# Two attention and GLU layers for one decode step: the first attention's V product made wide, its score mask and q block made one matmul each, and the places at the change of stage dealt anew

## The chip, the cores and the metric

The kernel runs on one core of one Trainium2 chip. The metric is the device time of one execution in microseconds (us). The core has five engines with a queue of their own each: TensorE (PE, with its weight loads shown apart as PEld), VectorE (DVE), ScalarE (ACT), GpSimd (POOL) and SyncE (SP), which here only issues transfers. Sixteen DMA engines move the data from HBM to the on-chip memory (SBUF). Matmuls write to PSUM, eight banks of 512 fp32 per partition.

## The reference

Four sequences, one new token each (x is 4 x 512), go through attention, GLU, attention, GLU, with the same weights and caches both times:

```python
W = min(4096, max(256, Sk // 4))            # 2048 of the 8192 cached places
q = (x @ wq).reshape(B, 1, 32, 128)          # 32 query heads, 8 key heads: 4 share one
scores = q . k[last W] * Dh ** -0.5
o = softmax(scores) . v[last W]
attn = o.reshape(B, 1, 4096) @ wo
glu = (sigmoid(g) * u) @ w_down              # g = x @ w_gate, u = x @ w_up, F = 1792
x = x + attn(layernorm(x)); x = x + glu(layernorm(x)); and both once more
```

All tensors are bf16. One pass needs K and V of the window, 16.8 MB each, wq and wo 4.2 MB each, and three GLU matrices of 1.8 MB each.

## The kernel before, in words

**Places.** SBUF holds 50 slots of 4 KB per partition (`arena`). Slots 0 to 31 hold K of all eight heads, four slots a head in two tiles (`kpair`): K is read once, turned in place on DVE and used by both attentions. The other 18 slots are nine tiles of 8 KB, through which everything else goes: wq, wo (four tiles, kept from the first attention to the second), V (two tiles a head, one for each pair of sequences) and the GLU's matrices. A tile is given back when its last reader is done (`done`), and the next load of the list takes it. Around the change from the first attention to the GLU and on to the second attention, loads of half a tile are used (`load_half`), and each has a fixed home in a table (`homes`): a half of the tiles named Y and Z (V of head 7), GA (first V tile of head 6), WQ (first tile of wq) or SP, which is the small scratch `side`. Parts of V of heads 6 and 7 and of wq stay for the second attention. One V tile of head 7 is parked in PSUM during the GLU: DVE transposes copy it there (`stash`, L578, and `stash_half`, L600) and back (L593, L606).

**Order.** All loads go out on SP's queue in one fixed order (`loads`, issued at L401); SP waits at each load until the last reader of its place is done, so a load that waits holds up all behind it. Every compute step is an operation of a planner (`_Plan`), with what it reads, writes and which PSUM banks it uses. `_schedule` orders the steps of each engine by estimated costs, and engines run their steps strictly in that order. From the end of the first GLU on, PE's steps keep the order in which they are written (`P.chain`).

**One head of the first attention.** DVE turns K in four pieces (L887). `q_unit`: four matmuls with a shifted eye `eyew` (L875) spread the head's q over a block, ACT copies it to `qbd` (L880). `softmax_unit`: four matmuls write the mask to four groups of 32 partitions of a bank (L905), 16 more add the scores (L916); DVE takes the maxima (L929 to L941), ACT the exponentials (L944). `turn_p`: one matmul permutes them (L957), ACT copies (L959), DVE transposes (L964) to `ebuf`. `sums_old`: POOL splits the sums into three bf16 parts (L973 to L977), PE spreads them (L983), DVE inverts (L990). `pv_unit`: 32 matmuls of 128 x 8 for each V tile, with V as the weights (L1006), so the first tile can be used and given back before the second lands; then DVE (L1014), PE (L1024), DVE (L1029), and `wo_unit` (L1195), 16 matmuls of 128 x 16.

**One head of the second attention, heads 7 to 1,** takes the wide path. `pv_wide`: 16 matmuls with the exponentials as weights and V streamed 512 wide (L1088), which need both V tiles; then on DVE a transpose (L1097), a reduction (L1102) and a shift (L1104), on POOL a sum and a product with the inverse sums (L1106, L1109); `o_back`: two small matmuls (L1123) and an ACT copy (L1129); `wo_wide`: four matmuls 512 wide (L1142), added up over the heads in one bank and turned back once (`wo_copy` L1169, `wo_back` L1179), or `wo_compact`: 16 small ones (L1158). The sums take one fp32 matmul (L1064) between POOL steps (L1059, L1069). The wide path's buffers lie in a slot that wq has left (`wide_buffers`).

**The GLU** multiplies with w_gate and w_up, four loads each (L1379), and with w_down (L1420, L1445).

Of the kernel before, what the change touches and what calls it, by code (L numbers as in the profile page):

```python
# [6 lines left out]
F32 = mybir.dt.float32  # L7
# [271 lines left out]
def build(nc, A_x, A_k, A_v, A_wq, A_wo, B_wg, B_wu, B_wd, out, cfg=None):  # L279
# [45 lines left out]
    with es:  # L325
# [12 lines left out]
        eyew = sb("eyew", [128, 224], BF16)  # L338
# [4 lines left out]
        msk_s = sb("msk_s", [128, 32], BF16)  # L343
# [178 lines left out]
        def load_wq(k):  # L522
# [3 lines left out]
            else:  # L526
                for i in (1, 0):
                    for c in range(i, NC):
                        load_half(("wq", c, k, i), wq_d[:, c, i * SLOT:(i + 1) * SLOT], "bw_4k", SLOT,
                                  (((Y, 0), (Y, 1), (WQ, 1), (WQ, 0)), (None, (WQ, 0), (GA, 0), (SP, 0)))[i][c])  # L530
# [23 lines left out]
        def load_glu(k):  # L554
            for nm, src, two in (("wg", wg_d, wg_p), ("wu", wu_d, wu_p)):
                if k == 0:
                    for c in range(NC):
                        load_half((nm, c, k), src[:, c, :], "bw_3k", F,
                                  (((WQ, 0), (GA, 0), (SP, 0), (Y, 0)), ((Y, 1), (Z, 0), (WQ, 0), (GA, 0)))[nm == "wu"][c])
# [3 lines left out]
            for n, (a, b) in enumerate(bounds_of(k)):  # L563
                if k == 0:
                    load_half(("wd", a, k), wd_d[:, a:b, :].rearrange("p k n -> p (k n)"), "bw_4k", (b - a) * D,
                              ((SP, 0), (Y, 0), (Y, 1), (Z, 0))[n])
# [42 lines left out]
        def load_v(h, bp, k, n_use):  # L609
            name = ("V", h, bp, k)  # L610
            tiles = {(HKV - 2, 0): ((GA, 0),), (HKV - 3, 1): ((Y, 0), (Y, 1))}.get((h, bp)) if k else None
# [20 lines left out]
        def keep_wq(s):  # L632
            hfree.add(s)
# [13 lines left out]
        P.op("gpsimd", "eyew0", 200.0, lambda g: g.memset(eyew[:], 0.0), w=[("eyew0",)])  # L647
# [4 lines left out]
        for jh in range(2):  # L652
            for bp in range(2):
                for i in range(2):
# [10 lines left out]
             lambda g: g.affine_select(msk_s[:, :].rearrange("p (i y) -> p i y", i=2),  # L665
                                       ones_f[:, :].rearrange("p (i y) -> p i y", i=2),
                                       [[1, 2], [0, NR]], ALU.is_equal, 0.0, base=-1, channel_multiplier=1),
# [15 lines left out]
             lambda v: v.tensor_reduce(eyew[:, 96:128], ident.rearrange("p (a j) -> p j a", a=4), AXX, ALU.max),  # L683
             r=[("e", 0), ("eyew0",)], w=[("eyew",)])
# [6 lines left out]
        ey = eyew[:, 96:128]  # L691
# [11 lines left out]
        P.op("vector", "selw", 100.0, lambda v: v.tensor_copy(selw[:, :], eyew[:, 96:96 + NB]), r=[("eyew",)], w=[("selw",)])  # L703
# [163 lines left out]
        def q_unit(tag, h, k2):  # L867
            hh = h % 4
            src = qh[32 * hh:32 * hh + 32, h // 4 * 64:h // 4 * 64 + 64].rearrange("p (x r) -> p x r", r=REP)
            dst = ps[:, CB, 0:256].rearrange("p (x y) -> p x y", y=NR)  # L870

            def e_qx(pe):
                last = None
                for a in range(4):
                    last = pe.matmul(dst[:, :, a * REP:(a + 1) * REP], eyew[32 * hh:32 * hh + 32, 96 - 32 * a:224 - 32 * a],  # L875
                                     src, start=True, stop=True)
                return last
            P.op("tensor", "qx" + tag, 250.0, e_qx, r=[("qh", h // 4), ("eyew",)], w=[("cb",)], banks=(CB,))
            P.op("scalar", "qe" + tag, c_act(256),
                 lambda a: a.copy(qbd[:, k2 * 256:(k2 + 1) * 256], ps[:, CB, 0:256]),  # L880
                 r=[("cb",)], w=[("q", k2)], banks=(CB,))
# [12 lines left out]
        def softmax_unit(tag, hk, wait=False, q=True, between=None):  # L894
# [7 lines left out]
            def e_m(pe):  # L902
                last = None
                for gi in range(4):
                    last = pe.matmul(ps[32 * gi:32 * gi + 32, bank, :], msk_s[:, :],  # L905
                                     msk_m[:, :].unsqueeze(1).broadcast_to([128, 256, 2]), start=True, stop=False)
                return last

            def e_s(pe):
                last = None if wait else e_m(pe)  # L910
                for cp in range(4):
                    for gi in range(4):
# [4 lines left out]
                                         kt[:, cp // 2, cp % 2, jh * NJ:(jh + 1) * NJ, :], start=False, stop=(cp == 3))  # L917
# [37 lines left out]
        def turn_p(L, tag, k2, pb, wide=False):  # L955
# [10 lines left out]
            if L == 0:  # L966
                sums_old(tag, k2)
# [70 lines left out]
        def wide_buffers(slots, op):  # L1038
# [15 lines left out]
            rest["op"] = op  # L1054

# [518 lines left out]
```

## Time and profile before

| | |
|---|---|
| median of 3 runs | 177.51 us (177.5 to 178.89) |
| the profiled execution | 177.0 us, of which the span of the instructions is 175.3 |
| read from HBM | 69.73 MB, 398 GB/s over the span |
| busy: PE, PEld, DVE, ACT, POOL | 105.7, 54.7, 104.4, 32.7, 22.2 us |
| matmuls | 1661, and as many weight loads |
| first attention: K transposes | 32 of 1205 ns |
| V products: L1006, L1088 | 576 matmuls, 18.2 us; 112 matmuls, 7.3 us |

In the profile, L12 is line 12 of the kernel before. A group of instructions is told as line, engine, operation, what it writes and reads, how often, and then busy time and mean duration. The page's section 2 cuts the span into 40 slices; a digit is the busy share in tenths. In the chain of work, each piece has its start, its length and what it was, followed back from the last instruction to whatever released it. A "DMA" piece is time in which the chain waited for a transfer. In answers by windows, the columns are the window, its length, the busy time and number of instructions of each engine, the granted PE clock, the DMA share and GB/s. In an answer on one line, the three numbers are the least, middle and greatest duration in ns, then the first and last start in us.

### The profile page before, as it was taken

The numbers are of one execution on the slowest core, as the hardware profiler recorded it, in microseconds if no ns is written. First come the engines' busy times: TensorE is split into PE (matmuls) and PEld (weight loads), VectorE is DVE, ScalarE is ACT, GpSimd is POOL, SyncE is SP. The second block draws the span as 40 slices with busy tenths as digits, with TensorE's granted clock in tenths as the row PEclk, the third lists the DMA queues.
The fourth block names the chain that finished last, engine by engine and source line by source line (L and its number), as shares of the span: only waits on it lengthen the run. The fifth ranks groups of instructions, "written<-read, shape, count | busy, mean of one in ns | idle before, by whom it ended". The sixth has DMA issues, their size and how long they took to land.

```text
span 175.3 us, 3927 instructions
## 1 busy us (share of the span) xinstructions
PE 105.7 (60%) x1661; PEld 54.7 (31%) x1661; DVE 104.4 (60%) x257; ACT 32.7 (19%) x87; POOL 22.2 (13%) x90
## 2 busy tenths in 40 slices
PE   0536246259566273661765456547977999776673
PEld 0203112014334041340445452142322444445321
DVE  6307997994957738378322381316299999751351
ACT  2002031322303003021030000100143455430011
POOL 6100010101101001010010000000011453442000
PEclk9999999999999999999999999999999999995555
DMA  5999999999999999999999999999999999999980
GB/s 188 426 426 426 426 419 424 408 421 423 419 419 412 420 424 426 421 405 427 419 419 415 415 400 407 402 410 403 394 413 404 423 419 424 421 416 423 419 344 25
DMA packets 12226, 70.00 MB, mean 399 GB/s; under 512 B 1320, under 2 KB 1328, under 8 KB 6064
## 3 DMA queue, kind: packets, MB, share of 16 engines
q1 hardware_dynamic: 12200, 69.74, 97.1%
q8 instruction: 13, 0.21, 0.5%
q14 instruction: 5, 0.04, 0.1%
q10 hardware_dynamic: 8, 0.00, 0.0%
HBM read 69.73 MB, written 0.00 MB: 398 GB/s over the span
## 4 chain that ended last, share of the span: by engine, by line
DMA 52%; DVE 24%; PE 19%; issue 2%; SPq 1%; ACT 0%; DVEq 0%
DMA arena<-in_A_v_cache_dram 20%; DMA arena<-in_B_w_down_dram 18%; DVE arena L887 12%; DMA arena<-in_A_wq_dram 10%; PE ps L916 8%; DMA arena<-in_B_w_gate_dram 5%; DVE small L929 3%; PE ps L905 3%; PE ps L1088 2%; DVE small L933 1%; DVE arena L593 1%; PE ps L1006 1%; DVE side L937 1%; PE ps L828 1%; DVE small L941 1%
## 5 line engine op out<-in xcount | busy, mean ns | idle before, releaser
L887 DVE STREAM_TRANSPOSE arena<-arena 128x1024 f32<-128x1024 f32 x32 | 37.0, 1205 | 0.1
L1006 PE MATMUL ps<-side,arena 128*128 128x8 bf16 x576 | 18.2, 168 | 14.1 <-DMA arena<-in_A_v_cache_dram 14.0
L916 PE MATMUL ps<-arena,side 128*32 128x512 bf16 x256 | 25.0, 524 | 0.1
L1006 PEld LDWEIGHTS ps<-side,arena 128*128 128x128 bf16 x576 | 16.7, 104 | 20.5 <-DMA arena<-in_A_v_cache_dram 18.8
L929 DVE TENSOR_REDUCE small<-ps 128x1 f32<-128x512 f32 x16 | 10.8, 676 | 17.6 <-PE ps L916 17.5
L944 ACT ACTIVATE side<-ps,small 128x512 bf16<-128x512 f32 x16 | 11.0, 687 | 36.8 <-PE ps L1024 18.3
L905 PE MATMUL ps<-small,msk_s 128*32 128x512 bf16 x64 | 8.4, 512 | 13.9 <-DVE arena L887 13.1
L880 ACT CAST side<-ps 128x256 bf16<-128x256 f32 x16 | 5.9, 370 | 34.4 <-PE ps L916 25.4
L959 ACT CAST side<-ps 128x512 bf16<-128x512 f32 x16 | 9.4, 586 | 10.8 <-PE ps L957 10.8
L916 PEld LDWEIGHTS ps<-arena,side 128*32 128x32 bf16 x256 | 8.2, 119 | 10.0 <-issue 7.2
L973 POOL CAST small<-small 128x1 bf16<-128x1 f32 x9 | 1.7, 188 | 76.1 <-ACT side L944 76.1
L957 PE MATMUL ps<-side,perm 128*128 128x512 bf16 x16 | 7.9, 494 | 5.2 <-ACT side L944 5.2
L828 PE MATMUL ps<-arena,xn 128*4 128x512 bf16 x60 | 7.5, 572 | 3.9 <-DMA arena<-in_A_wq_dram 3.6
L784 ACT ACTIVATE small<-ps 128x4 f32<-128x4 f32 x4 | 0.7, 174 | 48.1 <-PE ps L780 48.1
L1379 PE MATMUL ps<-arena,xn 128*4 128x448 bf16 x60 | 7.2, 549 | 3.3 <-DMA arena<-in_B_w_up_dram 1.5
L964 DVE STREAM_TRANSPOSE side<-side 128x256 f32<-128x256 f32 x16 | 6.9, 433 | 2.0 <-ACT side L959 1.8
L875 PE MATMUL ps<-side,eyew 32*128 32x64 bf16 x64 | 5.6, 217 | 3.4 <-ACT side L880 2.4
L1088 PE MATMUL ps<-arena,side 128*32 128x512 bf16 x112 | 7.3, 381 | 0.2 <-DVE small L941 0.2
L1014 DVE TENSOR_TENSOR onb<-ps,rinv 128x16 bf16<-128x16 f32 x9 | 1.7, 185 | 9.0 <-PE ps L1006 8.8
L905 PEld LDWEIGHTS ps<-small,msk_s 128*32 128x32 bf16 x64 | 1.7, 97 | 16.8 <-DVE arena L887 15.4
L1388 DVE STREAM_TRANSPOSE side<-ps 128x448 f32<-128x448 f32 x4 | 2.6, 650 | 7.3 <-PE ps L1379 7.3
L840 DVE STREAM_TRANSPOSE side<-ps 128x512 f32<-128x512 f32 x3 | 2.1, 716 | 7.9 <-PE ps L828 7.8
(123 smaller groups left out, 137.8 us busy)
## 6 DMA issues: line engine op xcount, KB each, us to landing
arena<-in_A_v_cache_dram SPq DMA_DIRECT2D x27, 1024.0 KB, 18.8
arena<-in_A_k_cache_dram SPq DMA_DIRECT2D x16, 1024.0 KB, 24.9
arena<-in_A_wq_dram SPq DMA_DIRECT2D x4, 1024.0 KB, 7.8
arena<-in_A_wo_dram SPq DMA_DIRECT2D x3, 1024.0 KB, 26.5
arena<-in_A_wq_dram SPq DMA_DIRECT2D x6, 512.0 KB, 6.3
arena<-in_B_w_up_dram SPq DMA_DIRECT2D x4, 448.0 KB, 6.1
arena<-in_B_w_gate_dram SPq DMA_DIRECT2D x2, 896.0 KB, 21.7
arena<-in_B_w_up_dram SPq DMA_DIRECT2D x2, 896.0 KB, 23.9
```

What stands on the lines that cost most here:

```text
L828: last = pe.matmul(ps[32 * hh:32 * hh + NB, qb, :], xn[:, c * NB:(c + 1) * NB], src[:, o + hh * 512:o + (hh + 1) * 512], start=(c == 0), s ...
L887: P.op("vector", "T%d_%d" % (h, t), c_dve(1024), lambda v, v32=v32: v.transpose(v32, v32), r=[("slot", 4 * h + t)], w=[("slot", 4 * h + t)])
L905: last = pe.matmul(ps[32 * gi:32 * gi + 32, bank, :], msk_s[:, :], msk_m[:, :].unsqueeze(1).broadcast_to([128, 256, 2]), start=True, stop= ...
L916: last = pe.matmul(ps[32 * gi:32 * gi + 32, bank, :], qbd[:, q0:q0 + 32], kt[:, cp // 2, cp % 2, jh * NJ:(jh + 1) * NJ, :], start=False, s ...
L929: lambda v: v.tensor_reduce(nmax[:, k2:k2 + 1], ps[:, bank, :], AXX, ALU.max),
L944: lambda a: a.activation(prow[:, :].rearrange("p (m x t) -> p m x t", x=32, t=2), ps[:, bank, :].rearrange("p (m t x) -> p m x t", x=32, t ...
L957: lambda pe: pe.matmul(ps[:, pb, :], perm[:, :], prow[:, :], start=True, stop=True),
L959: P.op("scalar", "pc" + tag, c_act(512), lambda a: a.copy(prow[:, :], ps[:, pb, :]), r=[("ppb", pb)], w=[("prow",)], banks=(pb,))
L964: P.op("vector", "pt" + tag, c_dve(256), lambda v: v.transpose(et, prow[:, :].bitcast(F32)), r=[("prow",)], w=[("e", k2)])
L1006: last = pe.matmul(ps[:, ob, bp * 8:bp * 8 + 8], src[:, j * 128:(j + 1) * 128], ev[:, j % 2, j % 16 // 2, x0:x0 + 8], start=(j == 0), stop ...
L1088: last = pe.matmul(ps[32 * g:32 * g + 32, ob, :], ew[:, g, mq, t], src.rearrange("p (m t d) -> p t m d", t=2, d=128)[:, t], start=(n == 0) ...
L1379: last = pe.matmul(ps[32 * g:32 * g + NB, gub[n], 0:NF], xn[:, c * NB:(c + 1) * NB], src[:, g * NF:(g + 1) * NF], start=(c == 0), stop=(c ...
```

## The change: what it does

- In the first attention, heads 0 to 6 take the wide V path (`pv_wide`, `sums`, `o_back`); head 7 keeps the old one. Heads 0 to 4 take `wo_wide` and are turned back once, behind head 4; heads 5 and 6 take `wo_compact`.
- The wide path's buffers in the first attention (`first_buffers`) lie in the first half of tile WQ, from the time that wq's first load has been used until head 6's wo (`give(base[WQ])`). Both parities of heads share most of them (`kk = 0`).
- The mask is one matmul over all 128 partitions (`msk_s` is 128 wide), and the q block is one matmul of 128 x 64 with `eye4`, followed by a product on DVE with the mask `maskp` in place of ACT's copy.
- WQ's first half is no longer free at the start of the GLU's loads, so the homes of wq's, w_gate's, w_up's, w_down's and two V loads are dealt anew. The order of the loads and their sizes stay.
- The stash of head 7's tile is tied to head 6's transpose, reduction and shift; head 6's wo comes behind head 7's `pm`.
- In the second attention, one part of wq is multiplied and the second q block made between the first mask and the first scores (`ahead`).

```diff
-                                  (((Y, 0), (Y, 1), (WQ, 1), (WQ, 0)), (None, (WQ, 0), (GA, 0), (SP, 0)))[i][c])
+                                  (((Y, 1), (WQ, 0), (WQ, 1), (GA, 0)), (None, (GA, 0), (Y, 0), (SP, 0)))[i][c])
...
-                                  (((WQ, 0), (GA, 0), (SP, 0), (Y, 0)), ((Y, 1), (Z, 0), (WQ, 0), (GA, 0)))[nm == "wu"][c])
+                                  (((GA, 0), (SP, 0), (Y, 0), (Y, 1)), ((WQ, 0), (Z, 0), (GA, 0), (Y, 0)))[nm == "wu"][c])
...
-                              ((SP, 0), (Y, 0), (Y, 1), (Z, 0))[n])
+                              ((SP, 0), (Y, 1), (WQ, 0), (Z, 0))[n])
...
-            tiles = {(HKV - 2, 0): ((GA, 0),), (HKV - 3, 1): ((Y, 0), (Y, 1))}.get((h, bp)) if k else None
+            tiles = {(HKV - 2, 0): ((Y, 0),), (HKV - 3, 1): ((Y, 1), (WQ, 0))}.get((h, bp)) if k else None
...
         def keep_wq(s):
-            hfree.add(s)
...
         def q_unit(tag, h, k2):
...
-                for a in range(4):
-                    last = pe.matmul(dst[:, :, a * REP:(a + 1) * REP], eyew[32 * hh:32 * hh + 32, 96 - 32 * a:224 - 32 * a],
-                                     src, start=True, stop=True)
...
-            P.op("scalar", "qe" + tag, c_act(256),
-                 lambda a: a.copy(qbd[:, k2 * 256:(k2 + 1) * 256], ps[:, CB, 0:256]),
+                 lambda pe: pe.matmul(dst, eye4[32 * hh:32 * hh + 32, :], src, start=True, stop=True),
...
+            P.op("vector", "qe" + tag, c_dve(256),
+                 lambda v: v.tensor_tensor(
+                     qbd[:, k2 * 256:(k2 + 1) * 256].rearrange("p (x a r) -> p x a r", a=4, r=REP),
+                     dst.rearrange("p (x r) -> p x r", r=REP).unsqueeze(2).broadcast_to([128, NR, 4, REP]),
+                     maskp[:, :].unsqueeze(1).unsqueeze(3).broadcast_to([128, NR, 4, REP]), ALU.mult),
...
             def e_m(pe):
-                for gi in range(4):
-                    last = pe.matmul(ps[32 * gi:32 * gi + 32, bank, :], msk_s[:, :],
-                                     msk_m[:, :].unsqueeze(1).broadcast_to([128, 256, 2]), start=True, stop=False)
+                return pe.matmul(ps[:, bank, :], msk_s[:, :],
+                                 msk_m[:, :].unsqueeze(1).broadcast_to([128, 256, 2]),
+                                 start=True, stop=False, skip_group_check=True)
...
+        def first_buffers(s, op):
+            f = slot_ap(s).bitcast(F32)
+            for k2 in range(2):
+                n = 0
+                for name, size in (("tv", 512), ("o32", 32), ("osh", 32), ("A", 128), ("mb", 64)):
+                    rest[name, k2] = f[:, n:n + size]
+                    n += size
...
         def attn_first():
...
+            first_buffers(base[WQ], named("q0_1_0")[0])
             for h in range(2):
                 front(h)()
+                sum_up(h)
             for h in range(HKV):
                 tag = "0.%d" % h
                 turn = front(h + 2) if h + 2 < HKV else None
+                if h < HKV - 1:
+                    pv_wide(tag, h, h % 2, v_tiles[(0, h)])
+                    if turn is not None:
+                        turn()
+                    if h == HKV - 2:
+                        give(SIDE)
+                    op = late.pop(("tr", tag))()
+                    if h < HKV - 3:
+                        wo_wide(tag, h, op, h % 2, h == 0, h == HKV - 4)
+                    else:
+                        wo_compact(tag, h, op, h % 2)
+                    if h == HKV - 2:
+                        give(base[WQ])
+                    if h == HKV - 4:
+                        wo_copy(0)
+                        wo_back(0, False)
+                    sum_up(h + 2)
+                    continue
                 if h == HKV - 1:
-                    oe, oq = named("oe0.%d" % (h - 1)), named("oq0.%d" % (h - 1))
-                    oe[0].deps.add(stash(stashed, (0, 1)))
-                    oq[0].deps.add(stash(stashed, (2,), oe))
-                    st = stash(stashed, (3,), oq)
+                    rd, sh = named("rd0.%d" % (h - 1)), named("sh0.%d" % (h - 1))
+                    rd[0].deps.add(stash(stashed, (0, 1), named("tv0.%d" % (h - 1))))
+                    st = stash(stashed, (2,), sh)
+                    st = stash(stashed, (3,), sh)
...
+                named("WO0.%d_%d" % (h - 1, h - 1))[0].deps.add(named("pm" + tag)[0])
...
+            def ahead():
+                q_mms(1, 0, OBS[1], (1,))
+                qx(1)
+
             qx(0)
-            score(0, lambda: q_mms(1, 0, OBS[1], (1,)))
-            qx(1)
+            score(0, ahead)
```

## The prediction

> **What bounds the kernel.** I read the page first: the slices and the queues.
>
> ```profile
> span 175.3 us, 3927 instructions
> ...
> PEclk9999999999999999999999999999999999995555
> DMA  5999999999999999999999999999999999999980
> ...
> q1 hardware_dynamic: 12200, 69.74, 97.1%
> q8 instruction: 13, 0.21, 0.5%
> q14 instruction: 5, 0.04, 0.1%
> ...
> DMA 52%; DVE 24%; PE 19%; issue 2%; SPq 1%; ACT 0%; DVEq 0%
> ```
>
> The sixteen DMA engines are full in 38 of 40 slices. Their packets take 97.1 + 0.6 = 97.7% of the span, 171.3 us; the rest is the head before the first packets and the tail after the last landing. No engine does half as much on the chain. Then the chain in order of time, around the change from attention to GLU:
>
> ```profile
> 61.03 1.71 PE ps L916 x14
> 62.73 0.96 PE ps L1006 x32
> ...
> 63.71 23.07 DMA arena<-in_A_v_cache_dram
> ...
> 86.83 1.03 PE ps L1006 x32
> ...
> 87.87 11.31 DMA arena<-in_A_v_cache_dram
> ...
> 99.20 1.33 DVE ps L578 x2
> ...
> 100.62 8.17 DMA arena<-in_B_w_gate_dram
> ```
>
> From 63.7 us on compute only hands back places: a load lands, PE uses it, the next load goes out 0.1 us later. So what counts is each load's **lead**: the landing of the load before it minus its own issue. The first load needs 4.80 us from issue (0.79) to landing, and later ones of its size land 2.49 apart, so 2.3 us are fixed; a load with a lead above 2.3 leaves no hole in the queue. Before, leads are over 15 us until 76, then 8.3 (V of head 6, second tile, issued 85.94), 7.0 (w_gate's fourth load, 100.62), 4.3 (w_up's third, 106.74) and 3.9 at the least (120.30 and 126.61). At the end the queue runs out raggedly:
>
> ```profile
> 166.00:168.00 2.00, 2.00 (x18) 0.60 (x10) 0.87 (x2) 0.59 (x4) 0.00 (x0) 0.50 1.01 422
> 168.00:170.00 2.00, 1.34 (x16) 0.38 (x16) 1.58 (x4) 0.13 (x1) 0.00 (x0) 0.50 0.92 371
> 170.00:172.00 2.00, 1.16 (x40) 0.88 (x44) 0.01 (x1) 0.00 (x0) 0.00 (x0) 0.50 0.35 131
> ```
>
> The last columns are DMA share and GB/s. From 168 there are (0.92 + 0.35) x 2 = 2.5 us of work left, so engines that ended together would be done at 170.5; the last landing is at 172.4. Up to 1.9 us of the end belongs to the engines that end last.
>
> **Part by part.** The loads keep their bytes, forms and order (69.74 MB): 0 us. What can change is leads, and what else runs on the DMA engines.
>
> *V wide, heads 0 to 6.* Each loses 64 matmuls (L1006, 2 x 1.02 us) and, behind them, L1014 0.18, L1024 0.28, L1029 0.23; it gains 16 matmuls like L1088 and, on DVE, L1097 0.70, L1102 0.43, L1104 0.18, on POOL L1106 0.26, L1109 0.67, then L1123 0.2 and L1129 0.18. L1088 stands only in the second attention, 1.05 us for 16; the 16 score matmuls, of the same form, tell what the first attention would pay:
>
> ```profile
> L916 PE MATMUL ps<-arena,side x144: 628/628/634, 21.1 to 125.9; 128*32 128x512 bf16 x144
> L916 PE MATMUL ps<-arena,side x112: 379/387/408, 127.4 to 149.2; 128*32 128x512 bf16 x112
> ```
>
> Up to 126 us the same matmul takes 628 ns, later 387, though the granted clock reads 9 throughout; sixteen take 1.93 and 1.10. So the wide V costs between 1.05 and 1.93, and I take 1.9, the row of its own stage. DVE gains 1.31 - 0.41 = 0.9 us a head here, less 0.07 for a smaller reciprocal.
>
> *q block.* Four matmuls (L875, 0.39) become one; the copy goes from ACT (L880, 0.37) to a DVE product of 256. L1014 and L1029 give 0.184 for 16 and 0.225 for 64 elements, so 0.39; bounds 0.23 (the 64) and 0.68 (L929's 512). I take 0.4. *Mask*: one 512-wide matmul for four that ran side by side (0.62 with their start, of which score takes over some): a gain of 0 to 0.3 on PE, taken as 0.1.
>
> DVE per head of the first attention: 4 x 1.205 + 0.68 + 0.33 + 0.25 + 0.21 + 0.43 + 0.25 + 0.41 = 7.4, then 8.6, against 4.5 MB x 2.48 = 11.2 us of loads. It fits, but K of head 7 (landed 79.26) is transposed later: in the new DVE order the maxima of head 6 and the V work of head 3 stand ahead of it, so its transposes end near 84.3 for 82.1 and its scores near 86.6. The V tile that the next step needs lands at 86.78, so this costs nothing; from there on I walk by hand, with landings as before:
>
> PV of head 4: 86.8 to 88.7; it frees both tiles at once. V6's second tile goes at 88.8, lead 94.21 - 88.8 = 5.4. Then DVE 0.70 + 0.43 + 0.18 to 90.1, POOL 0.93 to 91.2, L1123 to 91.5, turn (L957) 0.61 to 92.1, wo wide (four 512s, 0.60 as L828) to 92.7, sums to 93.2, and only then PV of head 5, whose V has been there since 91.73: ends 95.1. V7's second tile at 95.2: lead 99.18 - 95.2 = 4.0, for 8.8 before. The wo of heads 0 to 4 turned back once (L1179, 0.95 to 1.9) ends by 97.0; PV of head 6 to 98.9; w_gate 0 and 1 at 99.0, lead 104.28 - 99.0 = 5.3 (10.1 before: its place was free, now it is V6's).
>
> *Places anew, stash order.* WQ's first half is scratch until head 6's wo. w_gate 2 waits for two stash transposes (from 99.2, with head 7's reciprocal between them) and PV: 101.1, lead 5.4. Reduction and shift of head 6, then two more: w_gate 3 at 103.1, lead 4.5. w_up 0 waits for POOL's 0.93 and L1123: 103.4, lead 5.4. w_up 1 waits for the last stash: 105.2 for 104.90, lead 4.7. w_up 2 at 107.0, 4.0. w_up 3 waits for the third gate product in place of the second: 108.3 for 107.16, lead 112.15 - 108.3 = 3.9; w_down 0 behind it in SP's order, 108.6, 4.7. From there on places follow each other as before.
>
> *Second attention.* Score 0 now waits for a product on DVE and for the second q matmul: 127.0 for 126.6, lead 3.5. Later leads grow as before (6 to 25). DVE per unit goes from 3.3 to 3.7, still under the 4.97 that two V tiles take. At the end, the attention closes at 162.6, w_up's last piece lands at 168.10 and holds the GLU; the first half of its products ends at 166.6, so 1 us of delay there is free.
>
> All leads stay over 2.3, by 1.2 at the least: 0 us.
>
> *Instructions.* They come over the same DMA engines: 0.25 MB for 3927, 64 B each, at 0.6% of the span, 1.05 us. The change has 516 matmuls fewer, with their weight loads 1032 instructions, 66 KB: 1.05 x 66/250 = 0.28 us. It is nothing if it falls on engines that end early, and up to 1.9 if all of it is on those that end last (four packets of 16 KB, each 0.5% x 175.3 x 16 / 13 = 1.08 us of one engine). I take 0.3.
>
> **Sum.** The profiled execution took 177.0 (span 175.3 and 1.7 around it): 177.0 - 0.3 = 176.7. The median of the runs is 0.5 above the profiled one, so 177.2.
>
> **Rivals.**
> *A, a hole in the queue (slower).* V7's second tile now sits behind PE's wait for POOL (head 4's way back), a turn, wo and sums. For: its lead falls from 8.8 to 4.0, and 6.4 us of hand-overs were added up from rows of another stage. Against: with matmuls at 387 ns it would be 2 us earlier. It decides once that tile goes out after 99.18 - 2.3 = 96.9, 1.7 later than I reckon; each us beyond is one of the end. If the hand-overs cost half as much again (3.2), the hole is 1.5, and score 0's 3.5 may add 0.5: 179.2. Chance 0.16.
> *B, the second attention stays at 628 ns.* The switch at 126 followed 3.5 us of unbroken streaming; the change thins it by the masks and q matmuls. Then a unit takes 2.35 (mask and score) + 1.9 + 0.61 + 0.60 + 0.8 = 6.3 on PE, more than 4.97; eight from 124.9 end at 175 instead of 162.6: 177.2 + 12.4 - 2 of slack = 188. Against: at 628 ns PE is busier still, which brings the switch. Chance 0.02. The Trainium skill has this rule (TensorE: Matmul & The Clock Gate, Part 1: The HAM clock gate): half clock by default, released after about 3.4 us of sustained activity, taken back after an idle window. The two L916 rows agree with it; by that rule the wide V might also wake PE in the first attention, which would only lengthen the leads.
> *C, the fetches sat on the engines that end last (faster).* 177.2 + 0.3 - 1.9 = 175.6. Chance 0.06; the gain over 1% needs nearly all of it.
> *D, the change does less than it says*: V wide for seven heads needs tiles that land together. The new order has seven groups of 16 and five wo groups of 4, so I give this no chance of its own.
>
> **How the numbers follow.** Forecast 0.76 with its own range 176.3 to 178.2; A 0.16, B 0.02, C 0.06. A measurement here tells about 1%, 1.8 us. Faster 0.06, within 1% 0.78 (a small hole counts here), slower 0.16. The range, 176.2 to 179.3, takes in the highest run before (178.89) and A's price, and leaves out B, C and the larger holes of A, some 0.15 in all.
>
> **What would show it.** DMA share 9 in the same slices and q1 at 97%; fewer than 13 packets on q8; the issue of V7's second tile near 95 and of w_gate 0 near 99; score matmuls of 387 ns from about 127. Wrong would be: a slice of DMA under 9 between 95 and 130, or a last landing other than 170.5 to 172.4.

## The result, and the profile after

The changed kernel takes 179.65 us, median of 20 runs (178.39 to 180.9), against 177.36 for the kernel before in the same comparison (176.87 to 178.89): a ratio of 1.0114, with a 95% interval of 1.0086 to 1.0142. The forecast was 177.2 and its range ended at 179.3; the median lies above it. The profiled execution took 178.83, at the lower end of the 20.

The page of the changed kernel: size, granted clock, DMA share and GB/s in 40 slices, the queues, and the chain that ended last.

```profile
span 177.1 us, 2946 instructions
...
PEclk9999999999999555555585555555589999996558
DMA  5999999999999999999999999999999999999960
GB/s 182 424 427 427 420 426 422 413 418 418 424 422 414 422 420 424 420 412 423 416 427 422 400 405 388 379 356 415 404 392 420 424 420 420 426 416 420 416 264 7
...
q1 hardware_dynamic: 12200, 69.74, 96.4%
q8 instruction: 9, 0.15, 0.4%
...
DMA 36%; DVE 24%; PE 17%; SPq 15%; issue 3%; ACT 1%; POOL 1%; POOLq 0%; DVEq 0%; ACTq 0%
```

There are 981 instructions fewer, and 9 fetch packets on q8 for 13, close to what was worked out. The DMA row still reads 9 nearly everywhere, but slices 25 to 27 (106 to 120 us) move 388, 379 and 356 GB/s, where the same slices of the kernel before have 407, 402 and 410: too small a loss for the tenths. And DMA holds 36% of the chain for 52%.

Where the new chain ends, in order of time (start, length, engine, tile, line), first after, then before:

```profile
171.73 0.50 DVE onp L1451
172.24 0.54 DVE side L1435
172.80 0.23 DVE rinv L1453
173.03 0.14 issue
173.17 1.56 PE ps L1467 x56
```

```profile
146.35 25.46 DMA arena<-in_B_w_down_dram
171.82 0.04 issue
171.86 0.59 PE ps L1420 x8
172.45 0.03 issue
172.49 0.41 PE ps L1420 x6
```

Before, the last products wait for pieces of w_down as they land. After, all 56 run in one go: their other operand, the product of gate and up (call it h; L1453), was ready only at 173.03, where it had been at 170.01. The last landing is at 173.54 for 172.44, outside the 170.5 to 172.4 that the prediction had named. So both things moved: the transfers end 1.1 us later, and the arithmetic behind the second attention ends 3.0 us later and has become the end.

The score matmul of the prediction, now in the changed kernel, before and after the clock comes up at 130, and the last 6 us of the queue (columns: busy time of PE, PEld, DVE, ACT, POOL, then granted clock, DMA share, GB/s):

```profile
L914 PE MATMUL ps<-arena,side x160: 384/628/632, 21.6 to 129.1; 128*32 128x512 bf16 x160
L914 PE MATMUL ps<-arena,side x100: 377/394/628, 129.1 to 151.6; 128*32 128x512 bf16 x100
```

```profile
168.00:170.00 2.00, 1.71 (x17) 0.53 (x17) 0.14 (x1) 0.00 (x0) 0.00 (x0) 0.50 0.97 395
170.00:172.00 2.00, 2.00 (x22) 1.04 (x26) 1.35 (x4) 0.72 (x4) 0.00 (x0) 0.50 0.56 220
172.00:174.00 2.00, 1.33 (x48) 0.86 (x40) 0.99 (x3) 0.00 (x0) 0.00 (x0) 0.50 0.04 14
```

### The profile page after: what moved, and what is told of

Same layout as the page of the kernel before. It is cut to its first block, busy times and chain, and to the rows that moved or that the text cites. A ratio compares the mean times of both kernels' runs of the same rounds, so it can differ in the third digit from the quotient of the medians.

```text
span 177.1 us, 2946 instructions
## 1 busy us (share of the span) xinstructions
PE 106.9 (60%) x1156; PEld 44.1 (25%) x1156; DVE 116.5 (66%) x281; ACT 29.0 (16%) x79; POOL 27.5 (16%) x90
## 4 chain that ended last, share of the span: by engine, by line
DMA 36%; DVE 24%; PE 17%; SPq 15%; issue 3%; ACT 1%; POOL 1%; POOLq 0%; DVEq 0%; ACTq 0%
DMA arena<-in_A_v_cache_dram 26%; SPq L401 15%; PE ps L1111 6%; DMA arena<-in_A_wq_dram 4%; DVE arena L1120 4%; DMA arena<-in_B_w_gate_dram 3%; DVE small L928 3%; DMA arena<-in_B_w_down_dram 3%; DVE arena L887 3%; DVE side L963 2%; DVE arena L1125 2%; PE ps L914 2%; DVE side L936 2%; DVE small L932 1%; DVE arena L593 1%
## 5 line engine op out<-in xcount | busy, mean ns | idle before, releaser
L914 PE MATMUL ps<-arena,side 128*32 128x512 bf16 x256 | 25.2, 528 | 0.2 <-DVE side L877 0.2
L1111 PE MATMUL ps<-arena,side 128*32 128x512 bf16 x224 | 20.6, 504 | 4.5 <-DMA arena<-in_A_v_cache_dram 3.9
L903 PE MATMUL ps<-small,msk_s 128*128 128x512 bf16 x16 | 8.4, 525 | 15.8 <-DVE arena L887 9.4
L1120 DVE STREAM_TRANSPOSE arena<-ps 128x512 f32<-128x512 f32 x14 | 10.0, 712 | 7.4 <-PE ps L1111 5.9
L1129 POOL TENSOR_TENSOR arena<-arena 64x32 f32<-64x32 f32 x14 | 3.4, 243 | 52.5 <-DVE arena L1127 52.5
L1148 PE MATMUL ps<-small,arena 64*128 64x8 bf16 x28 | 2.9, 171 | 11.6 <-POOL arena L1132 9.9
L1080 POOL TENSOR_SCALAR arena<-sel_r,small 128x8 f32<-128x8 f32 x14 | 4.3, 305 | 35.3 <-ACT side L943 35.3
L914 PEld LDWEIGHTS ps<-arena,side 128*32 128x32 bf16 x256 | 6.5, 113 | 12.7 <-issue 10.2
L1111 PEld LDWEIGHTS ps<-arena,side 128*32 128x32 bf16 x224 | 6.4, 113 | 12.7 <-issue 10.7
L1132 POOL TENSOR_TENSOR arena<-arena 64x256 bf16<-64x256 f32 x14 | 9.3, 667 | 1.1
L877 DVE TENSOR_TENSOR side<-ps,small 128x256 bf16<-128x256 f32 x16 | 6.1, 382 | 1.2 <-PE ps L874 1.2
## 6 DMA issues: line engine op xcount, KB each, us to landing
arena<-in_B_w_gate_dram SPq DMA_DIRECT2D x2, 896.0 KB, 21.5
```

What stands on the lines that cost most here:

```text
L903: return pe.matmul(ps[:, bank, :], msk_s[:, :], msk_m[:, :].unsqueeze(1).broadcast_to([128, 256, 2]), start=True, stop=False, skip_group_c ...
L914: last = pe.matmul(ps[32 * gi:32 * gi + 32, bank, :], qbd[:, q0:q0 + 32], kt[:, cp // 2, cp % 2, jh * NJ:(jh + 1) * NJ, :], start=False, s ...
L1111: last = pe.matmul(ps[32 * g:32 * g + 32, ob, :], ew[:, g, mq, t], src.rearrange("p (m t d) -> p t m d", t=2, d=128)[:, t], start=(n == 0) ...
L1120: P.op("vector", "tv" + tag, c_dve(512), lambda v: v.transpose(tv, ps[:, ob, :]), r=[("pso", k2, 0), ("pso", k2, 1)] + hold, w=[("tv", kk) ...
L1132: lambda v: v.tensor_tensor(av[0:64, :].rearrange("p (x q e) -> p x q e", x=8, q=4), o32[0:64, :].rearrange("p (q x) -> p x q", x=8).unsqu ...
```

## The experiments

**A measure used throughout.** The bytes that q1 has delivered by a time t are compared with the time at which the first profile of the kernel before had delivered as many. The difference says by how many us the sixteen engines together are behind; that first profile itself stands at nothing by definition. The changed kernel is 0.2 ahead at 108, 0.21 behind at 112, 0.39 at 116, 0.81 at 120 and 0.67 at the end. The stretch as windows, after and then before:

```profile
110.00:112.00 2.00, 1.21 (x9) 0.24 (x9) 1.24 (x4) 0.72 (x4) 0.00 (x0) 0.50 0.97 340
...
114.00:116.00 2.00, 0.81 (x28) 0.74 (x25) 0.86 (x2) 0.00 (x0) 0.00 (x0) 0.50 0.96 371
116.00:118.00 2.00, 0.93 (x29) 0.77 (x27) 0.00 (x0) 0.00 (x0) 0.00 (x0) 0.50 0.99 327
```

```profile
110.00:112.00 2.00, 1.09 (x8) 0.21 (x8) 1.01 (x4) 0.65 (x4) 0.00 (x0) 1.00 1.03 402
...
114.00:116.00 2.00, 0.88 (x27) 0.82 (x28) 0.81 (x2) 0.00 (x0) 0.00 (x0) 1.00 1.03 409
116.00:118.00 2.00, 0.92 (x28) 0.75 (x26) 0.00 (x0) 0.00 (x0) 0.00 (x0) 1.00 1.03 409
```

**Theory 1**: the q block's product on DVE makes each unit of the second attention (the work of one head) longer, and the arithmetic becomes the end. **Theory 2**: the new places, above all w_up's fourth piece, which waits for the third gate product in place of the second, let the DMA engines run dry between 105 and 120. **Theory 3**: PE's clock comes up later. (hT in the expectations is h.)

### The product off DVE, in the second attention (a_act2)

The added lines, shortened:

```
+            if tag[0] == "2":
+                for a in range(4):   # on ACT, into the four interleaved parts of qbd
+                    a_.activation(qv[:, :, a], dst, ACTF.Copy, scale=maskp[:, a:a + 1])
```

> The changed kernel, but in the second attention the q block goes from PSUM to the block matrix by four scaled copies of 64 on ACT in place of one product of 256 on DVE (382 ns by the changed kernel's row L877). Nothing is left out. Theory 1 (DVE: eight products of 0.38 us lengthen the chain of DVE in the second attention, which then ends 3.3 us late, so that the last GLU waits for its operand and not for w_down): the second attention's last wo ends 2 to 3 us earlier than the changed kernel's 165.9, the last products wait for w_down again, and the time is 1.2 to 2 us under the changed kernel, 177.6 to 178.4. Theory 2 (places: w_up 3 waits for the third gate product, the DMA engines run partly dry between 105 and 120, and all after it is 1 us late): the last landing stays near 173.5 for 172.4 and the time at 178.4 or above. Theory 3 (PE's matmuls turn from 628 to 387 ns at 131 instead of 127): the time stays at 179 or above, since the mask and the q matmul are as thin as in the changed kernel.

178.04 us (10 runs, 177.4 to 179.01), a ratio to the kernel before of 1.0023 (0.9996 to 1.0051). h is ready at 171.02, and the chain is again the transfers':

```profile
DMA 51%; DVE 16%; SPq 14%; PE 14%; issue 2%; ACT 1%; POOL 0%; DVEq 0%; ACTq 0%
```

The last landing stays at 173.52, and the engines are 0.5 behind at 120. So in this pair of kernels 1.6 of the 2.3 us hang on that product. The 0.4 to 0.7 that is left, by the ratio or by the medians, is not clear of noise: the interval reaches below 1.

### The other parts, each alone (a_v, b_q, b_mq)

a_v is the changed kernel with the old mask and the old q block, so wide V, wo and places alone. b_q is the kernel before with the new q block alone, b_mq with q block and mask.

> The changed kernel with the old mask (four matmuls) and the old q block (four matmuls and ACT's copy): the wide V of the first attention, wo and the new places alone. Nothing is left out. Theory 1: no slower than before by more than 0.3 us, 177.0 to 177.7, the second attention's last wo near 162.6 to 163.4. Theory 2: the whole loss stays, 178.4 to 179.6, with DMA dips between 105 and 120 as in the changed kernel. Theory 3: matmuls of 387 ns from about 127 again, and the time as before.

> The kernel before with the new q block alone (old mask of four matmuls). Nothing is left out. Theory 1: the same loss as with the mask, 178.2 to 179.4. Theory 3: with four mask matmuls PE streams more, so it turns to 387 ns earlier than with the one mask matmul, and the loss shrinks to under 0.5 us. Theory 2: 177.0 to 177.6.

> The kernel before with the new mask and the new q block (one matmul each, product on DVE) and nothing else. Nothing is left out. Theory 1: it carries most of the loss, second attention's last wo 2 to 3 us later than 162.6, time 178.2 to 179.4. Theory 2: no loss, 177.0 to 177.6, since the places are the old ones. Theory 3: the loss is here too, but with matmuls of 387 ns from about 131; if they come at 127 and the loss is here, theory 3 is out.

a_v took 179.64 (177.94 to 180.38; 1.0111, 1.0079 to 1.0142), where theory 1 wanted 177.0 to 177.7: a clear miss. Its end is the transfers'; they lose 0.4 us up to 120 and another 1.2 between 124 and 134, which the changed kernel's profile did not do. So there is a second thin stretch.

b_q took 181.71 (1.0241, 1.0201 to 1.0281) and b_mq 182.15 (1.0257, 1.0219 to 1.0294), more than any theory had. The windows of b_q show why:

```profile
132.00:134.00 2.00, 1.53 (x17) 0.46 (x14) 1.17 (x3) 0.58 (x1) 0.00 (x0) 0.50 0.25 102
134.00:136.00 2.00, 1.94 (x26) 0.71 (x18) 1.70 (x6) 0.00 (x0) 0.70 (x3) 0.85 0.93 283
```

At 132 to 134 the queue is nearly empty (102 GB/s). In these two kernels the product of unit 1 stands on DVE behind unit 0's maxima and four transposes from the stash (L593, about 2.4 us); the second scores wait for it, and V of head 4's second tile waits for the scores: it goes out at 132.79, with a lead of 1.0, where the kernel before has 128.50 and 6.2. Some 0.7 of these 4.3 us is the clock: PE had waited 3.69 us for the product, the granted clock reads 0.50 from 131.2 to 134.6, and the 16 score matmuls take 1.76 us for 1.10. Neither run has the thin stretch at 109 to 118; both have the old places.

### The order that the change brought with it (b_qa)

b_q with the changed kernel's `ahead`, which puts unit 1's product before the first scores:

```
+            def ahead():
+                q_mms(1, 0, OBS[1], (1,))
+                qx(1)
             qx(0)
-            score(0, lambda: q_mms(1, 0, OBS[1], (1,)))
-            qx(1)
+            score(0, ahead)
```

> The kernel before with the new q block (one matmul and a DVE product), and with the second q matmul group and the second q block put between the second attention's first mask and first score, as the changed kernel does. Narrow V, old mask, old places. Nothing is left out. Against the run with the new q block alone (181.71) it moves one product ahead of the maxima of unit 0 and the four unstash transposes. Theory 1 (each unit of the second attention is about 0.35 us longer on DVE, and the attention ends 2.5 to 3 us later than w_up needs it): the hole at 132 goes, V of head 4's second tile goes out at 129.5 to 130.5, and the product alone costs 1.0 to 1.8 us at the end: 178.4 to 179.2, with the last GLU's hT after 172.5 and the w_down products in one go after the last landing. If the cost of the new q block were the queue's hole alone: 177.2 to 177.8, the end again set by w_down's landings.

178.71 (178.21 to 180.81; 1.0070, 1.0035 to 1.0104), inside theory 1's interval. That tile goes out at 129.56 and the hole is gone: the order alone is worth 3.0 us. Some 1.1 us are left, in the old kernel too. This run does not split them: h is ready at 172.97, 3.0 later than before, and the last matmul ends 0.75 after the last landing (173.77), where it ended 0.43 after it before; but the transfers are 0.9 behind as well, most of it lost at 124 to 136.

### The places alone, and one pair of them exchanged (b_places, a_act, a_act_swap, a_act2_swap)

b_places is the kernel before with the four new tables of places. a_act has the ACT copies in both attentions. The two swaps exchange the places of w_gate's second and third piece, so that w_up's fourth waits for the second gate product again:

```
-                                  (((GA, 0), (SP, 0), (Y, 0), (Y, 1)), ((WQ, 0), (Z, 0), (GA, 0), (Y, 0)))[nm == "wu"][c])
+                                  (((GA, 0), (Y, 0), (SP, 0), (Y, 1)), ((WQ, 0), (Z, 0), (GA, 0), (Y, 0)))[nm == "wu"][c])
```

> The kernel before with the new table of places alone (the four tables of homes for wq, w_gate, w_up, w_down and for the two pinned V tiles); narrow V, wo, mask and q block as before. Nothing is left out. Theory 2 (the places make the holes at 105 to 120: w_up's fourth piece waits for the third gate product): the mean progress of the DMA engines falls 0.4 to 0.8 us behind that of the kernel before between 108 and 120 and stays there; 177.8 to 178.5. Theory 2b (the holes there come from the later hand-overs of the wide V, and the places only from its order): no loss against the kernel before in that stretch beyond 0.2 us; 177.2 to 177.6. Theory 1 (q product) expects nothing here: 177.4.

> The changed kernel with the q block of both attentions made by four scaled copies of 64 on ACT in place of the DVE product. Nothing is left out. The run that did so in the second attention alone gave 178.04. Theory 1 with theory 2 (in the first attention the product lies beside the loads; what is left is the places): the same as that run, 177.7 to 178.3, the last landing again near 173.5. If the product's time in the first attention delays the hand-overs of V and so makes the holes after 108: a loss of under 0.3 us at 120 and 177.3 to 177.7.

> The changed kernel with the q block on ACT in both attentions, and with the places of w_gate's second and third piece exchanged, so that w_up's fourth piece waits for the second gate product, as before the change, and the second w_gate piece in its turn waits for the stash transposes (about 101.7 for 99.3). Nothing is left out. Theory 2: w_up's fourth piece goes out at 107.3 to 107.7 (lead near 4.8) for 108.5, the loss by 120 is under 0.4 us, 177.3 to 177.8. If the loss comes from the whole chain of late hand-overs and not from that piece: the loss stays at 0.5 to 0.8 us, or comes earlier (at 102 to 108, from the second w_gate piece), 177.8 to 178.6.

> The changed kernel with the q block of the second attention alone on ACT (that gave 178.04) and the places of w_gate's second and third piece exchanged. Nothing is left out. Theory 2 (the thin queue of 109 to 118 comes from w_up's fourth piece and costs what it loses): no loss before 120, and 177.3 to 177.7. If what is won there is lost again in the thin stretch of 124 to 134, as in the run with ACT in both attentions: 178.0 to 179.0, no better than without the exchange.

| run | median (range) | ratio, 95% | behind at 108 | at 120 | at 136 |
|---|---|---|---|---|---|
| b_places | 178.16 (176.89 to 179.38) | 1.0018, 0.9983 to 1.0053 | 0.18 | 0.41 | 1.32 |
| a_act | 178.76 (177.84 to 180.10) | 1.0077, 1.0038 to 1.0116 | -0.23 | 0.55 | 1.91 |
| a_act_swap | 179.02 (178.04 to 180.24) | 1.0076, 1.0041 to 1.0110 | 0.04 | 0.02 | 1.61 |
| a_act2_swap | 178.78 (177.97 to 180.09) | 1.0077, 1.0046 to 1.0108 | 0.73 | 1.18 | 1.92 |

In a_act_swap w_up's fourth piece goes out at 107.56 for 108.49 and the stretch of 108 to 120 loses nothing. So theory 2's place is right. But it is no cure: what is kept there is lost at 124 to 134, and in a_act2_swap the hole moves ahead to 104 to 108, behind w_gate's second piece. b_places has the late piece too (108.43) and loses only 0.2 in that stretch, where the changed kernel lost 1.0; its time lies in theory 2's interval, its loss near theory 2b's, and its ratio can't be told from 1. Two things differ. The landing, which is that of the last engine, lies further behind the mean progress in the changed kernel: 1.8 us at w_gate's fourth piece, against 1.4 in b_places and in the kernel before. And w_up's third piece, just ahead of the late one, has a lead of 3.93 for 4.28. a_act, which takes still more off DVE, missed both its intervals and is slower than a_act2 by 0.7: its profile loses 1.4 us between 120 and 136. None of these versions beats the kernel before.

### A double dose of the product (a_dose)

Each product of the second attention is issued twice.

> The changed kernel with each DVE product of the q block in the second attention issued twice, the second waiting for the first and writing the same values. Nothing is left out. Theory 1 (in the changed kernel the DVE chain of the second attention, and no longer the transfers, sets the end): every product added there comes out at the end: 8 x 0.38 = 3.1 us, up to 3.5 with the wait of the second for the first, so 182.5 to 183.3, hT near 176, the last landing within 1 us of the changed kernel's 173.5. Theory 2 (the transfers set the end and the units have cover): less than 1 us more, 179.5 to 180.6.

180.21 (4 runs, 179.98 to 181.0; 1.0156, 1.0111 to 1.0201). Theory 1's 182.5 to 183.3 missed, and the number lies in the interval of theory 2, but its profile is that of theory 1 at half the size: the last landing is at 173.05, h ready at 174.24, the last matmul ends at 176.05, 3.0 after the landing. A unit of the changed kernel on DVE, whole, from one product to the next:

```profile
138.18 0.36 DVE L877 TENSOR_TENSOR side<-ps,small 128x256 bf16<-128x256 f32 x1
138.46 0.67 DVE L928 TENSOR_REDUCE small<-ps 128x1 f32<-128x512 f32 x1
139.06 0.70 DVE L1120 STREAM_TRANSPOSE arena<-ps 128x512 f32<-128x512 f32 x1
139.79 0.41 DVE L1125 TENSOR_REDUCE arena<-arena 128x32 f32<-128x128 f32 x1
140.24 0.18 DVE L1127 COPY arena<-arena 64x32 f32<-64x32 f32 x1
140.45 0.45 DVE L963 STREAM_TRANSPOSE side<-side 128x256 f32<-128x256 f32 x1
140.92 0.33 DVE L932 COPY small<-small 64x1 f32<-64x1 f32 x2
141.29 0.26 DVE L936 SCALAR_TENSOR_TENSOR side<-small,maskr 128x32 f32<-128x32 f32 x1
141.58 0.21 DVE L940 TRANSPOSE_TENSOR_REDUCE small<-side 128x1 f32<-128x32 f32 x1
141.71 0.16 DVE L1087 RECIPROCAL arena<-ps 64x8 f32<-64x8 f32 x1
141.79 0.36 DVE L877 TENSOR_TENSOR side<-ps,small 128x256 bf16<-128x256 f32 x1
```

It has no wait: 3.61 us from product to product, all work. The same distance is 3.33 before and 4.02 with the double dose. So each dose comes out in every unit, 0.29 and then 0.40 us. Why 1.74 in all for the second one, and not 3.1? In the changed kernel two units take 3.82 and 4.10, and in the dose 4.03 and 4.02. Three rows of one operation, the changed kernel's, the double dose's and that of a_act2 (shortest/median/longest ns of eight), tell the reason:

```profile
L936 DVE SCALAR_TENSOR_TENSOR side<-small,maskr x8: 252/258/721, 128.5 to 154.4; 128x32 f32<-128x32 f32 x8
```

```profile
L943 DVE SCALAR_TENSOR_TENSOR side<-small,maskr x8: 252/252/253, 128.3 to 155.9; 128x32 f32<-128x32 f32 x8
```

```profile
L946 DVE SCALAR_TENSOR_TENSOR side<-small,maskr x8: 250/252/300, 128.3 to 151.5; 128x32 f32<-128x32 f32 x8
```

In those two units it takes 0.44 and 0.72 us in place of 0.25. POOL's product of 64x256 (L1132, 0.67) runs at the very same time, from 148.26 and 152.36; the second product moves the two apart. The changed kernel thus pays 0.7 us for a meeting on top of the product's own time, and the dose gets it back. And only six of the eight products stand between the first unit's bias and the last one's: 6 x 0.40 - 0.7 = 1.7, and 1.74 was measured (27.62 for 25.88 us). The profiles are 1.35 us apart in time (180.18 for 178.83); the medians only 0.6, since that of the changed kernel lies in the upper of its two groups, of which next.

### More executions of both kernels (after_2 to after_5, before_2)

The changed kernel's 20 runs lie in two groups, 178.4 to 178.8 (8) and 179.5 to 180.9 (12), and the first profile is one of the lower. The marks set down for more profiles:

> The changed kernel once more, for a second profile of it: its runs lie in two groups, 178.4 to 178.8 and 179.5 to 180.9, and the first profile is one of the lower group. Nothing is left out. Theory 1: in the upper group too hT comes after 172.5, and the DVE units of the second attention take 3.6 us each; a run of the upper group loses the rest either in the thin stretch of 124 to 134 (mean progress 1 us or more behind the first profile there) or in matmuls that stay at 628 ns beyond 130.

> The kernel before once more, for a second profile of it: the first one is of 177.0, at the low end of its runs (176.83 to 179.02). Nothing is left out. If the loss of 0.7 to 1.8 us between 124 and 134 that the other kernels show is chance of one execution as much as theirs, a profile of 177.5 or more shows part of it here too (mean progress 0.3 to 1.2 us behind the first profile from 134 on); if it is theirs alone, this profile follows the first within 0.2 us throughout.

> The changed kernel, a third profile. Nothing is left out. If its time is 179.5 or more: theory 2 wants the mean progress of the DMA engines 1.2 to 2 us behind the kernel before from 136 on, with the step between 124 and 134; theory 3 (clock) wants 512-wide matmuls at 628 ns beyond 130.5 and units longer than 3.62 us on DVE. If it is under 179: as the first two, 0.6 to 0.9 us behind and units of 3.62.

> The changed kernel, a fourth profile; the same marks as for the third.

> The changed kernel, a fifth profile; the same marks as for the third.

All in us from the span's start but the time; "first maxima" is the start of unit 0's in the second attention, "last bias" the end of the last unit's L940.

| execution | time | behind at 120 | at 136 | last landing | first maxima | last bias | h ready | last matmul |
|---|---|---|---|---|---|---|---|---|
| before | 177.00 | 0 | 0 | 172.44 | 126.62 | 151.63 | 170.01 | 172.87 |
| before_2 | 177.52 | 0.02 | 0.71 | 172.84 | 126.71 | 151.72 | 170.38 | 173.27 |
| after_2 | 178.30 | 0.66 | 0.85 | 173.21 | 127.20 | 154.57 | 172.67 | 174.17 |
| after | 178.83 | 0.81 | 0.71 | 173.54 | 127.44 | 154.91 | 173.02 | 174.69 |
| after_4 | 179.33 | 0.60 | 2.25 | 174.25 | 128.21 | 155.62 | 173.73 | 175.20 |
| after_3 | 179.97 | 1.11 | 1.16 | 173.18 | 127.70 | 155.12 | 174.27 | 175.76 |
| after_5 | 180.02 | 1.03 | 1.29 | 172.94 | 127.80 | 155.22 | 174.38 | 175.89 |
| a_act2 | 178.16 | 0.48 | 0.59 | 173.52 | 127.23 | 152.09 | 171.02 | 173.94 |
| a_dose | 180.18 | 0.71 | 0.69 | 173.05 | 127.23 | 156.44 | 174.24 | 176.05 |

In the five executions of the changed kernel the last matmul ends 1.5 to 1.7 after h, in both of the kernel before 2.9 after it. Time goes with h, not with the last landing: the two slowest have the two earliest landings. That is theory 1's end in all five. Theory 3 is out: the clock comes up at 129.3 to 130.3 in the three quicker ones and at 127.5 and 127.6 in the two slowest. What delays h differs. after_4, between the two groups, starts the second attention 0.8 to 1.0 later than the two quick ones, since wq's last pieces landed later (128.49 for 127.06 to 127.72). after_3 and after_5, of the upper group, start 0.3 to 0.6 later and lose another 1.0 between the last bias and h, shown here by the windows of after_3 and then of after:

```profile
154.00:156.00 2.00, 1.38 (x14) 0.67 (x18) 0.98 (x6) 1.06 (x4) 0.57 (x2) 0.70 1.01 422
156.00:158.00 2.00, 2.00 (x17) 1.03 (x9) 0.80 (x2) 0.35 (x2) 0.00 (x0) 0.50 1.05 430
```

```profile
154.00:156.00 2.00, 1.58 (x23) 0.87 (x24) 0.87 (x5) 0.90 (x4) 0.57 (x2) 1.00 1.00 418
156.00:158.00 2.00, 1.18 (x11) 1.05 (x9) 1.71 (x5) 0.82 (x2) 0.59 (x2) 1.00 1.02 420
```

The granted clock reads 0.50 from 154.8 to 158.2, and the 16 matmuls of a V (L1111) take 1.92 us there in place of 1.04. None of the marks that were set down had this: the clock came up early and then fell back. after_5 has the same fall, at 154.9. The times between the changes of the granted clock are multiples of 3.4 us in every profile, and where they lie differs: the 3.4 us before the fall begin at 151.4 and 151.5 in these two, at 149.8 to 150.8 in the other three. PE is busy 1.56 and 1.54 us in them, and 1.99 to 2.45 in the others, where the clock stays. A DVE that needs 3.6 us a unit leaves PE such thin places. The Trainium skill (TensorE: Matmul & The Clock Gate, Part 1: The HAM clock gate) says that the clock is taken back after an idle window of about 3.4 us, and that the windows run freely. The trace agrees with the fall and with its coming in two executions of five; PE was not wholly idle in that window, and how much work keeps the clock is not shown. In before_2 the clock falls at 156.2, but there h (170.38) is 2.5 us ahead of the last w_down landing (172.84) and nothing is lost.

before_2 is also the test of chance that its expectation set down: it loses 0.7 us between 124 and 134 against the first profile of the same program (177.52 for 177.00). The five profiles of the changed kernel lose 0.0 to 1.4 there. So a part of what single profiles show in that stretch, those of the other versions too, is the execution's and not the version's.

## Why the prediction was wrong

**Right.** The walk through the first attention and the GLU: V of head 6's second tile at 88.97 (88.8 forecast), V of head 7's at 94.52 (95.2), w_gate's pieces at 98.87, 99.25, 101.73 and 103.16 (99.0, 99.0, 101.1, 103.1), w_up's at 103.59, 105.39, 107.28 and 108.49 (103.4, 105.2, 107.0, 108.3), V of head 5 at 127.43 (127.0). The product took 0.38 (0.4 taken). The 512-wide matmul of the wide V takes 634 ns in the first attention and 16 of them 1.9, and the clock comes up at 130. A, B and C did not happen: at V of head 7's tile there is no hole, the clock rose, and no gain from fewer fetches can be seen. A's price, 179.2, is near the result by accident. One reading was loose, without effect: not all leads are over 15 us until 76, those of the second to the seventh load are 4.3 to 13.8.

**The step that failed first: "DVE per unit goes from 3.3 to 3.7, still under the 4.97 that two V tiles take".** The units do go to 3.62. But they are not paced by the landings, and were not before either. After, then before, the windows of 129 to 153, and the matmuls of the first half of head 0's V:

```profile
129.00:153.00 24.00, 20.43 (x246) 7.55 (x238) 22.71 (x68) 8.50 (x22) 8.18 (x24) 0.98 1.01 417
...
160.23 0.96 PE L1003 MATMUL ps<-side,arena 128*128 128x8 bf16 x32
```

```profile
129.00:153.00 24.00, 21.21 (x301) 9.40 (x301) 21.50 (x68) 11.09 (x32) 9.23 (x26) 1.00 1.01 416
...
156.92 0.97 PE L1006 MATMUL ps<-side,arena 128*128 128x8 bf16 x32
```

DVE is busy 22.7 of the 24 us, with no wait on another engine, for 21.5 and one wait of 1.0. Since a unit is shorter than 4.97, the units eat up a stock of landed tiles, and meet the landings only at the last one: in the kernel before, V of head 3 is used 2.3 us after its second tile landed, of head 1 1.2 after, and the first half of head 0's, at 156.92, 0.05 after (156.87). In the changed kernel that half is used at 160.23, 3.1 after it landed (157.13). Nothing there absorbs a longer unit. Six products in the loop at 0.29, the meeting with POOL (0.7) and a start 0.8 later are 3.2; the last bias came 3.3 later and h 3.0. **"1 us of delay there is free"** was about right in size: in the kernel before h could have come 1.2 later (170.01 and the 1.7 for all products in one go, against 172.87). The delay was 3.0, and 3.0 - 1.2 = 1.8 is what the first profile lost (178.83 for 177.00). The 0.4 a unit that the prediction had should have been summed over the eight units, 3.2 us, and set against that 1 us. By the medians this step is worth 1.6 us (a_act2 against the changed kernel), with the clock's fall in it, which two of five profiles show. That price holds for this pair alone: the versions whose transfers end later (a_act, the two swaps, a_v) are only 0 to 0.9 under the changed kernel, though the second attention has no such product in them either.

**The second: "a load with a lead above 2.3 leaves no hole in the queue".** The lead was counted to the landing of the load before, and that is the landing on the last of sixteen engines. At w_gate's fourth piece it lies 1.4 us behind the mean progress (the time at which q1 had delivered as many bytes) before and 1.7 to 2.1 in the five profiles after; engines that are ahead of the mean run dry while the lead still reads 3.8. Behind the hole, at w_down's pieces, the distance is down to 0.9 to 1.2: those that were ahead have lost it. Take this distance off the lead, and w_up's third and fourth piece have 2.3 to 2.7 us in the eight profiles that lose 0.7 to 1.2 from 108 to 120 (the changed kernel's five, a_act, a_act2, a_dose). They have 2.8 and 2.3 in a_v, which loses 0.3, 2.9 and 2.6 in b_places (0.2), 2.6 and 3.4 in a_act_swap (nothing), 3.0 and 3.7 in b_qa (nothing); and w_gate's second piece, with 2.2 in a_act2_swap, costs 0.7. So the 2.3 was about right, and the point from which the cover was counted was wrong. The order of these runs speaks for it, but no run moves the distance alone, the records don't name the engine, and one loss does not fit: 0.5 at 116 to 120 in a_act2_swap, where no piece is under 2.9. What it is worth at the end is open: a_act2 against the kernel before is 0.4 to 0.7, not clear of noise. Leads of 3.5 to 4.0 had been called safe "by 1.2 at the least".

**The base.** The 0.3 taken for fewer fetches was not seen, and the range's top, 179.3, came from A, with a hole as its one price; a late end by arithmetic had no case of its own.

**Still open.** Why the stretch of 124 to 134 loses nothing in one execution and 1.6 in another with the same issue times (127.43 and 127.42 for V of head 5 in the changed kernel and in a_act_swap), beyond the chance that before_2 shows; why a_v, which has neither product nor new mask, is as slow as the whole change; and so how much of b_places' wide spread is the places'. The parts do not add up: a_act2 is 0.5 above the kernel before, a_v, which has less of the change, 2.1.

## What to carry to other kernels

An engine whose work per round is under the transfer's time per round can still set the end: look whether it runs without gaps over the rounds, multiply the added time by their number, and set that against the slack at the end. Count a queue's cover from the mean progress of its engines, not from the landing, which is the last one's: here the two were 1.4 to 2.1 us apart. When a step moves to another engine, put it into the order of that engine first: the same product cost 4.2 us behind a row of transposes and 1.1 ahead of them.

## What was not expected of the hardware

A fetch of instructions is one packet of 16 KB, 0.9 to 1.1 us long in most cases. In the changed kernel's first profile head 0's last V tile landed at 160.46 behind a fetch at 157.5, 3.33 after the tile before it, where such tiles follow each other by 2.49. That the fetch did it is not shown: in after_3 and after_5 one at 157.9 and 157.8 left the distance at 2.47 and 2.48.

A DVE operation of 0.25 us with two inputs from on-chip memory took up to 0.72 beside a POOL product. The Trainium skill has that (GPSIMD Engine Reference, 8. Key points): POOL shares its interfaces to that memory with DVE, and contends with DVE instructions that have two inputs there. The trace agrees, 0.44 and 0.72 for 0.25. It adds that the operation is held and not slowed: in the eight profiles that have the q block's product on DVE once (the changed kernel's five, b_q, b_mq, b_qa) the two overlap 40 times, and each time the DVE operation ends 0.05 us after POOL's product; it takes 0.25 to 0.26 where POOL's has 0.2 left to run, and longer only where it has more. Moving a neighbour by 0.4 us takes it away.
